# A retention layer with a gated MLP on one core: q decayed in its natural layout, one activation table at first, b_spatial as one row, and a new order of all work

## The chip, the core and the metric

The kernel runs on one core of one Trainium2 chip. The core has five engines, each of which works through its own queue in order: TensorE (matmuls and transposes, "PE" in the profile, with its weight loads as "PEld"), VectorE ("DVE"), ScalarE ("ACT"), GpSimd ("POOL") and SyncE ("SP", which here only issues DMAs). Data lies in HBM, in the on-chip SBUF, and in eight PSUM banks of 128 x 512 fp32 into which TensorE writes. The metric is the device time in microseconds (us), median over runs.

## The reference

Four batches, eight heads, 768 tokens, head size 64. Each head has a decay `lam` between 0.97 and 0.99. The first half is causal linear attention with decay; its output, with the heads laid side by side (512 wide), is the input `x` of a gated MLP that mixes tokens.

```python
# attention, per head: out_i = sum over j <= i of lam**(i-j) * (q_i . k_j) * v_j
# (the reference does it in blocks of 64 with a running state kv_state)
h = np.maximum(x @ w_in, 0.0)                    # 512 -> 1024
u, v = h[..., :512], h[..., 512:]
v_n = (v - mean(v)) / np.sqrt(var(v) + 1e-06)    # per token, over 512
v_s = np.einsum('ts,bsd->btd', w_spatial, v_n) + b_spatial[None, :, None]
out = (u * v_s) @ w_out                          # 512 -> 512
```

`w_spatial` is 768 x 768 and mixes all tokens of a batch. So no product with `w_spatial` can be finished before the attention, the first product and the normalisation of all 768 tokens of that batch are done.

## The kernel before

**Tiling.** A step n = 0..11 is 256 tokens of one batch (three steps a batch). Its q, k and v are 512 KB loads each (`load`, lines 191 to 194); a partition holds two neighbouring tokens. There are three buffers each for q, k and v, so the load of step n+3 waits until step n has been read. A step is two chunks c = 0, 1 of 128 tokens; heads are worked on in four pairs, in halves i (or x) = 0, 1.

**The decay** is split: k is multiplied by lam to the power (384 - t), q by lam to the power (t - 384), so the scores need only a 0/1 triangle, and the state in PSUM bank 7 is accumulated without being scaled. The factors are exp of log(lam) times a position. They exist in two forms: `lv` and `lqn` with tokens on partitions (for the natural layout), and `lq` with tokens along the free axis (for the transposed layout).

**The order is written out by hand**: the string `ORDER` (lines 16 to 84) is a list of tokens `name.arguments.engine`, and each token issues one helper's instructions at once; engine letters are T (TensorE), D (VectorE), A (ScalarE), P (GpSimd) and S (SyncE). Each engine's queue is the subsequence of its tokens, so a token that waits holds back all later tokens of its engine. Numbers behind the step are the PSUM banks. The tokens, in the order in which a step uses them:

| token | what it does | lines |
|---|---|---|
| lam, LB, LN, LL, LX, LT | load lam, spread it over partitions with a matmul, logarithm, exponents `lv`/`lqn`, the 12 rows of `lq` | 196 to 227 |
| one, FL | a tile of ones; k matmuls of ones into a bank, whose result nobody uses (filler) | 264 to 270 |
| LQ, LK, LV | load q, k, v of a step | 272 to 279 |
| KM, QM | decayed k (`kc`), decayed q (`qc`) in the natural layout, half a step each | 297 to 301 |
| QC | q copied to bf16 without decay (`qc`) | 284 to 287 |
| TK, TQ, EK, EQ | transposes on TensorE into a bank; eviction to `kT`, `qT`. EQ multiplies by `lq` | 317 to 337 |
| DK, DQ | the same transposes done by DMA | 303 to 309 |
| SC, MK, VC, KV, SS | scores, their mask into `a_sb`, v to bf16, state, state to SBUF | 311, 345 to 375 |
| AV, FN, EX | attention output for a chunk, one-element read between, eviction to `xT` | 377 to 419 |
| PV, EV, BN, RA, RD, VN | v half of x @ w_in, relu, statistics, sqrt, reciprocal, normalised `vn` | 421 to 454 |
| PU, EU | u half, transposed; relu into `uT` | 456 to 469 |
| WI, WS, WO, BS | loads of w_in (two halves), w_spatial (two halves), w_out on POOL's queue, cast to bf16 on the way; b_spatial copied to all 128 partitions on SP's | 247 to 261 |
| GT | POOL reads one element of a loaded q, k or v buffer, which holds POOL's queue until that load has landed | 244 |
| WT, EW | w_spatial transposed: `wt_sb` | 471 to 481 |
| GP, PW, GM | bias into a bank, the spatial product on top of it (6 matmuls of 384 columns), times `uT` into `gT` | 483 to 495 |
| PO, EO, ST | last product, eviction, 256 KB store; PH, EH, SH the same for half a tile | 497 to 522 |

In the order before, q of steps 0 to 4 is copied (QC) and gets its decay at the eviction of its transpose (EQ with `lq`); from step 5 on it is decayed in its natural layout (QM) and transposed by DMA (DQ). Steps 0 to 4 of k are decayed naturally and transposed on TensorE, later ones by DMA.

Of the kernel before, what the change touches and what calls it, by code (L numbers as in the profile page):

```python
# [25 lines left out]
FN.1.2.4.A AV.1.1.2.4.T LV.4.S EX.1.0.2.D EQ.2.1.5.D EX.1.1.4.A FL.13.256.1.0.T PV.1.0.1.T EX.0.0.3.D SS.1.1.D  # L26
PV.0.1.6.T EV.0.1.6.A PV.1.1.0.T EV.1.1.0.A KM.3.0.P KM.3.1.P QC.3.2.P GT.2.2.P WO.P EV.1.0.1.D BN.1.0.D
BN.0.1.D TK.2.0.2.T BN.1.1.D PV.0.0.5.T VC.3.P FL.3.256.4.0.T TK.2.1.4.T EK.2.1.4.D EK.2.0.2.A SC.2.0.0.1.T
MK.2.0.0.1.D FL.2.256.3.0.T SC.2.1.3.4.T MK.2.1.3.4.D EV.0.0.5.A RA.1.A BN.0.0.D RA.0.A RD.1.D LV.5.S RD.0.D
PU.1.0.6.T PU.1.1.2.T KV.2.0.T SS.2.0.A EU.1.0.6.A AV.2.0.0.1.T FN.2.0.1.D VN.0.0.D VN.0.1.D PU.0.1.3.T  # L30
EU.0.1.3.A KM.4.0.P AV.2.1.0.1.T EX.2.0.0.A EX.2.1.1.D GP.0.0.0.4.A EU.1.1.2.A GP.0.0.1.5.A PU.0.0.6.T VN.1.1.D
VN.1.0.D EU.0.0.6.D PV.2.0.3.T KM.4.1.P EV.2.0.3.A BN.2.0.D PV.2.1.0.T EV.2.1.0.A BN.2.1.D WT.0.0.1.T WT.1.0.2.T
EW.1.0.2.A EW.0.0.1.D RA.2.A RD.2.D VN.2.0.D WT.2.0.6.T EW.2.0.6.D PU.2.0.3.T GP.0.2.0.0.A PU.2.1.2.T VN.2.1.D
PW.0.0.0.4.T EU.2.0.3.A EU.2.1.2.A WT.1.1.1.T EW.1.1.1.A WT.2.1.6.T EW.2.1.6.A GP.0.3.0.3.D GM.0.0.0.4.D
GP.0.1.1.2.A PW.0.2.0.0.T GM.0.2.0.0.D GP.0.1.0.4.A WT.0.1.1.T EW.0.1.1.D PW.0.3.0.3.T TK.3.2.6.T EK.3.2.6.A
TQ.3.2.0.T PW.0.1.0.4.T GM.0.1.0.4.D EQ.3.2.0.D PW.0.1.1.2.T GM.0.1.1.2.D GM.0.3.0.3.D PW.0.0.1.5.T GM.0.0.1.5.D
KV.3.0.T SC.3.0.0.1.T MK.3.0.0.1.D SC.3.1.2.3.T MK.3.1.2.3.D GP.0.2.1.4.A PW.0.2.1.4.T TK.4.2.6.T QC.4.2.A
# [50 lines left out]
def kernel(  # L88
# [84 lines left out]
    def bank(b):  # L173
        return ps[:, b]
# [387 lines left out]
```

## Time and profile before

| | us |
|---|---|
| median of 3 runs (148.59 to 150.53) | 149.34 |
| span of the profiled execution, first to last instruction | 147.9 |
| PE busy / PEld / DVE / ACT / POOL in that span | 137.0 / 90.1 / 114.9 / 82.1 / 46.7 |
| chain that ended last: PE / DVE / ACT / issue / DMA / POOL | 81% / 6% / 4% / 4% / 1% / 1% |
| first matmul of PV (L424) / of PW (L488) | 21.77 / 36.47 |
| end of the last matmul / end of the span | 144.2 / 147.9 |
| HBM read and written | 24.77 MB and 6.29 MB |

The groups of the page give, for each source line and shape, the number of instructions, the engine's busy time and the mean duration of one. A TensorE matmul's listed duration includes a pipeline's depth, so the rate of a stream is read from the chain, where 4 PV matmuls take 0.86 us and 30 PW matmuls 4.88 us. Rows of waits name the instruction that waited, how long, and what ended it.

### The profile page before, as it was taken

The page shows a single profiled execution, that of the slowest core. Times are in us where ns is not written, and L with a number is a line of the kernel's source. Part 1 is how long each engine was busy: PE and PEld are TensorE (multiplying, and loading weights), DVE is VectorE, ACT ScalarE, POOL GpSimd, SP SyncE. Part 2 cuts the span into 40 slices and gives each one's busy share as a digit, 9 for nine tenths or more (in the row PEclk, how much of TensorE's full clock was granted, in tenths as well). Part 3 has the DMA queues.
Part 4 walks back from the last instruction along what each step waited for, and adds up shares of the span by engine and source line. Part 5 has one row for each costly group of instructions (what it writes and reads, how often), then busy time and mean ns, then how long its engine had stood idle before and what let it go on. Part 6 is the DMA issues. An engine that isn't in the chain of part 4 may idle for free.

```text
span 147.9 us, 4771 instructions
## 1 busy us (share of the span) xinstructions
PE 137.0 (93%) x2019; PEld 90.1 (61%) x2032; DVE 114.9 (78%) x216; ACT 82.1 (56%) x165; POOL 46.7 (32%) x59
## 2 busy tenths in 40 slices
PE   4999899999199999999999899999999999999990
PEld 2688675768076755556656647657665565666530
DVE  4458958988956998799998968797795899696720
ACT  3886635598066473786663367987424446742041
POOL 7594562019700080226041800780732000000000
PEclk9999999999999999999999999999999999999999
DMA  3999999999999005999998999999999579200524
GB/s 95 347 347 345 231 279 219 217 295 289 242 246 274 5 20 135 278 334 251 198 216 242 244 139 337 339 197 260 296 250 173 181 295 340 81 0 4 206 101 189
DMA packets 58376, 32.30 MB, mean 218 GB/s; under 512 B 15858, under 2 KB 55282, under 8 KB 58354
## 3 DMA queue, kind: packets, MB, share of 16 engines
q1 hardware_dynamic: 55968, 29.23, 74.2%
q0 software_dynamic: 2384, 2.75, 11.0%
q8 instruction: 16, 0.26, 0.7%
q14 instruction: 6, 0.05, 0.1%
q10 hardware_dynamic: 2, 0.00, 0.0%
HBM read 24.77 MB, written 6.29 MB: 210 GB/s over the span
## 4 chain that ended last, share of the span: by engine, by line
PE 81%; DVE 6%; ACT 4%; issue 4%; DMA 1%; POOL 1%; POOLq 0%
PE ps L488 21%; PE ps L424 13%; PE ps L499 12%; PE ps L462 11%; PE ps L269 6%; PE ps L399 4%; PE ps L352 4%; PE ps L369 4%; PE ps L321 3%; PE ps L390 2%; DVE a_sb L357 2%; DVE st L439 1%; DMA out_dram<-o_sb 1%; ACT uT L429 1%; ACT L220 1%
## 5 line engine op out<-in xcount | busy, mean ns | idle before, releaser
L488 PE MATMUL ps<-wt_sb,vn 128*128 128x384 bf16 x192 | 33.8, 326 | 3.0 <-DVE wt_sb L180 3.0
L291 POOL TENSOR_TENSOR kc<-k_in,lv 128x512 bf16<-128x512 f32 x18 | 19.1, 1072 | 39.2 <-DMA k_in<-in_k_dram 17.9
L357 DVE TENSOR_TENSOR a_sb<-ps,m 128x1024 bf16<-128x1024 f32 x24 | 28.7, 1215 | 2.6 <-PE ps L352 2.6
L488 PEld LDWEIGHTS <-vn 128*128 128x128 bf16 x192 | 18.2, 98 | 15.3 <-DVE vn L453 4.3
L462 PE MATMUL ps<-xT,win_sb 128*128 128x256 bf16 x192 | 23.5, 273 | 0.0
L424 PE MATMUL ps<-win_sb,xT 128*128 128x512 bf16 x92 | 22.6, 379 | 0.2
L499 PE MATMUL ps<-wout_sb,gT 128*128 128x512 bf16 x83 | 21.7, 380 | 0.7 <-issue 0.3
L494 DVE TENSOR_TENSOR gT<-ps,uT 128x384 bf16<-128x384 f32 x32 | 16.6, 550 | 6.3 <-PE ps L488 5.5
L462 PEld LDWEIGHTS <-win_sb 128*128 128x128 bf16 x192 | 18.1, 98 | 3.9
L439 DVE BATCH_NORM_STATS2 st<-vh 128x6 f32<-128x512 bf16 x24 | 16.5, 686 | 3.3 <-ACT vh L429 3.1
L178 ACT ACTIVATE ps<-bsp 128x384 f32<-128x384 f32 x26 | 12.5, 493 | 9.5 <-DVE gT L494 6.4
L291 POOL TENSOR_TENSOR qc<-q_in,lqn 128x512 bf16<-128x512 f32 x11 | 11.9, 1087 | 17.2 <-DMA q_in<-in_q_dram 10.3
L178 ACT ACTIVATE o_sb<-ps 128x512 f32<-128x512 f32 x18 | 10.5, 596 | 11.0 <-PE ps L499 10.4
L429 ACT ACTIVATE vh<-ps 128x512 bf16<-128x512 f32 x19 | 11.3, 595 | 8.8 <-PE ps L424 8.8
L269 PE MATMUL ps<-ones 128*128 128x256 bf16 x86 | 13.8, 309 | 2.0 <-DVE ones L265 1.5
L424 PEld LDWEIGHTS <-xT 128*128 128x128 bf16 x96 | 9.3, 98 | 9.5
L499 PEld LDWEIGHTS <-gT 128*128 128x128 bf16 x92 | 8.4, 98 | 9.1
L453 DVE TENSOR_SCALAR vn<-vh,mv,rstd 128x512 bf16<-128x512 bf16 x24 | 13.5, 592 | 0.2
L178 ACT ACTIVATE xT<-ps 128x512 bf16<-128x512 f32 x15 | 8.5, 595 | 7.4 <-PE ps L399 7.4
L178 ACT ACTIVATE s_sb<-ps 128x256 bf16<-128x256 f32 x17 | 6.5, 380 | 8.9 <-PE ps L369 8.8
L269 PEld LDWEIGHTS <-ones 128*128 128x128 bf16 x86 | 8.7, 109 | 4.3 <-DVE ones L265 1.5
L429 ACT ACTIVATE uT<-ps 128x512 bf16<-128x512 f32 x17 | 9.9, 588 | 1.7 <-PE ps L462 1.7
(72 smaller groups left out, 172.9 us busy)
## 6 DMA issues: line engine op xcount, KB each, us to landing
k_in<-in_k_dram SPq DMA_DIRECT2D x12, 512.0 KB, 6.1
q_in<-in_q_dram SPq DMA_DIRECT2D x12, 512.0 KB, 6.0
v_in<-in_v_dram SPq DMA_DIRECT2D x12, 512.0 KB, 6.7
out_dram<-o_sb SPq DMA_DIRECT2D x23, 256.0 KB, 2.7
wsp_raw<-in_moe_w_spatial_dram POOLq DMA_DIRECT2D x2, 576.0 KB, 11.4
win_sb<-in_moe_w_in_dram POOLq DMA_DIRECT2D x2, 512.0 KB, 9.9
wout_sb<-in_moe_w_out_dram POOLq DMA_DIRECT2D x1, 512.0 KB, 8.9
bsp<-in_moe_b_spatial_dram SPq DMA_DIRECT2D x1, 384.0 KB, 14.2
```

Of the source, the lines that this page charges most:

```text
L178: nc.scalar.activation(out=o, in_=i, func=AF.Copy)
L269: nc.tensor.matmul(out=bank(b)[:, 0:w], lhsT=ones[:, 0:P], rhs=ones[:, 0:w], start=(new == 1 and i == 0), stop=True, skip_group_check=True)
L291: vec(e).tensor_tensor(out=dst[n % NCA][:, u].rearrange("p u m o d -> p o (u m) d"), in0=src[n % NIN].rearrange("p (o u) m d -> p o u m d" ...
L357: nc.vector.tensor_tensor(out=a_sb[n % NA][:, i].rearrange("p o w j x -> p o w (j x)"), in0=ps[:, b0:b1 + 1:b1 - b0].rearrange("p o (w y) ...
L424: nc.tensor.matmul(out=bank(b), lhsT=x[:, slot(c, g)], rhs=win_sb[:, g, DH:DFF], start=(g == 0), stop=(g == NCH - 1))
L429: nc.scalar.activation(out=o, in_=i, func=AF.Relu)
L439: nc.vector.bn_stats(out=st6[p2][:, t], in_=vh[p2][:, t])
L453: vec(e).tensor_scalar(out=vn[p2][:, t], in0=vh[p2][:, t], scalar1=mv[p2][:, t, 0:1], scalar2=rstd[p2][:, t:t + 1], op0=ALU.subtract, op1= ...
L462: nc.tensor.matmul(out=pu[:, f2].rearrange("p (c x) -> p c x", c=2), lhsT=win_sb[:, g, f * P:(f + 1) * P], rhs=x[:, slot(0, g):slot(1, g) ...
L488: nc.tensor.matmul(out=bank(b)[:, 0:HW], lhsT=vn[bb % 2][:, s, f * P:(f + 1) * P], rhs=wt_sb[:, s, i * HW:(i + 1) * HW], start=False, stop ...
L494: nc.vector.tensor_tensor(out=gT[bb % 2][:, f, cols], in0=bank(b)[:, 0:HW], in1=uT[bb % 2][:, f, cols], op=ALU.mult)
L499: nc.tensor.matmul(out=bank(b), lhsT=gT[bb % 2][:, f, t * P:(t + 1) * P], rhs=wout_sb[:, f, :], start=(f == 0), stop=(f == NCH - 1))
```

## The change

It does four things. q is decayed in its natural layout in all twelve steps: QC, LT, `pos`, `lq` and `llrow` are gone, QM takes QC's place, and EQ becomes a plain copy that ScalarE can do too. One ScalarE table set that holds both logarithm and exponential is loaded before the logarithm (`tab.0.A`), and the set with the square root by a token of its own (`tab.1.A`). b_spatial is loaded as one row of 3 KB (BR) and spread over the partitions by two fp32 matmuls against a row of ones (BB), evicted by BE. And the whole order, with all bank numbers, is a new one; the fillers go from 86 matmuls of 256 columns to 13 of 512.

```diff
+    def c_tab(e, j):
+        nc.scalar.preload_act_table_set("sqrt_and_others" if j else "natural_log_exp_and_others")
+    def c_row(e):
+        nc.vector.memset(one_row, 1.0)
...
-    def b_sp(e):
-        nc.sync.dma_start(out=bsp, in_=moe_b_spatial.unsqueeze(0).to_broadcast((P, S)))
+    def b_r(e):
+        {"S": nc.sync, "A": nc.scalar}[e].dma_start(out=brow, in_=moe_b_spatial.unsqueeze(0))
+    def b_b(e, i, b):
+        nc.tensor.matmul(out=bank(b)[:, 0:HW], lhsT=one_row, rhs=brow[:, i * HW:(i + 1) * HW], start=True, stop=True)
+    def b_e(e, i, b):
+        copy(e, bsp[:, i * HW:(i + 1) * HW], bank(b)[:, 0:HW])
...
     def e_q(e, n, x, b):
-        nc.vector.tensor_tensor(out=qT[n % NTR][:, part(x)].rearrange("p u m x -> p (u m x)"),
-                                in0=quad(b)[:, part(x)].rearrange("p u m x -> p (u m x)"),
-                                in1=lq[:, n % NR, part(x)].rearrange("p u m x -> p (u m x)"), op=ALU.mult)
+        copy(e, qT[n % NTR][:, part(x)].rearrange("p u m x -> p (u m x)"),
+             quad(b)[:, part(x)].rearrange("p u m x -> p (u m x)"))
```

The order up to the first products with w_spatial, before and after:

```diff
-one.D lam.A LK.0.S msk.P mkc.D FL.6.256.0.1.T LB.0.T LN.0.A posk.P LL.D LX.A KM.0.0.D pos.P idn.P
-FL.11.256.1.1.T TK.0.0.1.T KM.0.1.P FL.5.256.2.1.T TK.0.1.2.T LQ.0.S QC.0.1.D TQ.0.1.3.T LT.0.A QC.0.0.P
-TQ.0.0.4.T EQ.0.0.4.D LT.1.A EQ.0.1.3.D LK.1.S KM.1.1.P FL.13.256.5.1.T TK.1.1.5.T EK.0.0.1.A SC.0.0.3.4.T
-EK.0.1.2.A LQ.1.S QC.1.0.P EK.1.1.5.A GT.1.1.P WI.0.P KM.1.0.D LV.0.S SC.0.1.0.1.T LV.1.S TK.1.0.6.T EK.1.0.6.A
-FL.1.256.2.0.T TQ.1.0.2.T LQ.2.S LK.2.S QC.1.1.P FL.11.256.5.0.T TQ.1.1.5.T MK.0.0.3.4.D EQ.1.0.2.D MK.0.1.0.1.D
-VC.0.A FL.3.256.6.0.T KV.0.0.T AV.0.0.3.6.T SS.0.0.A FN.0.3.6.A LV.2.S QC.2.1.P BS.S LK.3.S GT.1.2.P WI.1.P
-EQ.1.1.5.D SC.1.1.0.1.T SC.1.0.4.5.T MK.1.0.4.5.D KV.0.1.T SS.0.1.A KM.2.0.P GT.2.1.P WS.0.P LQ.3.S LT.2.A
-AV.0.1.3.6.T LV.3.S LK.4.S VC.1.D FL.13.256.2.0.T KV.1.0.T LQ.4.S SS.1.0.A FL.5.256.2.0.T KV.1.1.T KM.2.1.P
-LK.5.S MK.1.1.0.1.D AV.1.0.2.4.T QC.2.0.A TQ.2.1.5.T EX.0.1.6.D WS.1.P TQ.2.0.0.T EQ.2.0.0.D LQ.5.S VC.2.P
...
+lam.A idn.P row.D msk.P LB.4.T tab.0.A LN.4.A LQ.0.S LK.0.S LK.1.S LQ.1.S one.D FL.4.512.0.1.T posk.P LL.D LX.A
+mkc.D LV.0.S BR.S FL.2.512.4.0.T QM.0.0.P QM.0.1.D TQ.0.0.0.T KM.0.0.D LV.1.S KM.0.1.D TK.0.0.4.T TQ.0.1.2.T
+TK.0.1.1.T EQ.0.1.2.D EK.0.1.1.D SC.0.1.2.3.T EK.0.0.4.A EQ.0.0.0.A KM.1.0.P LQ.2.S KM.1.1.D QM.1.1.P
+MK.0.1.2.3.D TK.1.0.1.T TK.1.1.4.T SC.0.0.0.5.T MK.0.0.0.5.D FL.2.512.6.1.T WI.0.P LK.2.S FL.2.512.2.0.T
+BB.1.6.T EK.1.1.4.A VC.0.A AV.0.0.2.3.T KV.0.0.T VC.1.P LV.2.S QM.1.0.D LK.3.S SS.0.0.D TQ.1.1.0.T EQ.1.1.0.D
+TQ.1.0.5.T EK.1.0.1.A FN.0.2.3.A AV.0.1.2.3.T EX.0.0.2.A QM.2.1.P QM.2.0.P SC.1.1.0.1.T LV.3.S EQ.1.0.5.D
+SC.1.0.4.5.T BE.1.6.D EX.0.1.3.A MK.1.0.4.5.D KV.0.1.T SS.0.1.A KV.1.0.T SS.1.0.A FL.2.512.3.0.T TQ.2.1.3.T
+MK.1.1.0.1.D BB.0.4.T TQ.2.0.0.T FL.1.512.5.0.T KM.2.1.D EQ.2.0.0.A EQ.2.1.3.A AV.1.0.5.6.T FN.1.5.6.A GT.2.1.P
+WI.1.P KM.2.0.D KV.1.1.T TK.2.1.2.T TK.2.0.1.T EK.2.1.2.D GT.1.1.P VC.2.P AV.1.1.5.6.T EK.2.0.1.D SC.2.1.0.2.T
+SC.2.0.1.3.T BE.0.4.A EX.1.0.5.A SS.1.1.A EX.1.1.6.A PV.0.1.4.T LQ.4.S MK.2.0.1.3.D MK.2.1.0.2.D eps.D
+EV.0.1.4.A PV.0.0.5.T PV.1.0.3.T BN.0.1.D LQ.3.S EV.1.0.3.A tab.1.A KV.2.0.T AV.2.0.2.6.T WS.0.P PV.1.1.0.T
+EV.0.0.5.D FN.2.2.6.D SS.2.0.D BN.1.0.D AV.2.1.2.6.T PU.1.1.1.T GP.0.2.0.5.A EV.1.1.0.A EX.2.1.6.A EX.2.0.2.D
+KM.3.1.P KM.3.0.P PV.2.0.4.T GT.2.2.P WS.1.P PV.2.1.0.T EV.2.0.4.A TK.3.2.3.T PU.2.0.6.T BN.1.1.D BN.0.0.D
+RA.1.A RD.1.D VN.1.1.D VN.1.0.D WT.2.0.2.T WT.0.0.4.T LK.4.S RA.0.A RD.0.D EW.0.0.4.D VN.0.1.D VC.3.P BN.2.0.D
+EU.1.1.1.A EK.3.2.3.A PU.1.0.3.T EU.2.0.6.A EV.2.1.0.A QM.4.0.P GT.1.2.P QM.4.1.P KV.3.0.T PU.0.1.6.T WT.1.0.0.T
+BN.2.1.D EW.1.0.0.D PU.0.0.1.T EW.2.0.2.A RA.2.A LK.5.S TQ.4.2.2.T PU.2.1.0.T RD.2.D VN.2.1.D EU.1.0.3.A
+VN.0.0.D WT.1.1.4.T GP.0.1.0.3.A EU.0.1.6.A EU.0.0.1.A EQ.4.2.2.D EU.2.1.0.A VN.2.0.D PW.0.2.0.5.T GM.0.2.0.5.D
+GP.0.0.0.1.D PW.0.1.0.3.T WT.0.1.2.T WT.2.1.5.T WO.P GP.0.3.1.6.A QM.3.0.P QM.3.1.P LQ.5.S LV.4.S GM.0.1.0.3.D
...
```

In the middle of batch 1 the new order has on POOL, in a row, `QM.6.0 KM.7.1 QM.7.0 KM.7.0 VC.7` and then `QM.8.0 QM.8.1 KM.8.0 KM.8.1`; VN of steps 3 to 5 stands on VectorE among them. The last stores are those of the two halves of tile 5 of batch 3 (`PH EH SH`), where before they were those of whole tiles.

More of the change, by code (lines that the diff above doesn't have):

```diff
@@ L150 @@
     bsp = sb([P, S], FP32, "bsp")
+    brow = sb([1, S], FP32, "brow")
     ones = sb([P, 512], BF16, "ones")
@@ L215, in l_l @@
                                 in1=posk.unsqueeze(2).broadcast_to((P, NR, H, 2)), op=ALU.mult)
-        for o in range(2):
-            nc.vector.tensor_copy(out=llrow[row(o)], in_=loglam[row(o), 4 * o:4 * o + 4])
     def l_x(e):
@@ L221, in l_x @@
         nc.scalar.activation(out=lv, in_=lv, func=AF.Exp)
-    def l_t(e, r):
-        for u in range(4):
-            nc.scalar.activation(out=lq[:, r, u].rearrange("p m x -> p (m x)"),
-                                 in_=posq[:, r].rearrange("p m x -> p (m x)"), func=AF.Exp,
-                                 scale=llrow[:, u:u + 1])
     def c_ident(e):
@@ L240, in c_mask2 @@
             nc.vector.tensor_copy(out=m01[rows], in_=mfull[rows, :, :, rows])
-        nc.vector.memset(eps_t, 1e-6)
-        nc.vector.memset(one_row, 1.0)
     def after(e, x, n):
@@ L522, in st_o @@
         eng.dma_start(out=out[bb, t * P:(t + 1) * P, :], in_=o_sb[(bb * NT + t) % NO])
-    ops = dict(GT=after, one=c_ones, FL=f_l, FN=f_n, lam=c_lam, posk=c_posk, pos=c_pos, LB=l_b, LN=l_n, LL=l_l, LX=l_x, LT=l_t, idn=c_ident, msk=c_mask, mkc=c_mask2, WI=w_in, WS=w_sp, WO=w_out, BS=b_sp,
-               LK=ld_k, LQ=ld_q, LV=ld_v, KM=k_m, QM=q_m, DK=d_k, DQ=d_q, QC=q_c, VC=v_c, TK=t_k, TQ=t_q, EK=e_k, EQ=e_q,
+    ops = dict(GT=after, one=c_ones, FL=f_l, FN=f_n, lam=c_lam, posk=c_posk, tab=c_tab, row=c_row, eps=c_eps, LB=l_b, LN=l_n, LL=l_l, LX=l_x, idn=c_ident, msk=c_mask, mkc=c_mask2, WI=w_in, WS=w_sp, WO=w_out, BR=b_r, BB=b_b, BE=b_e,
+               LK=ld_k, LQ=ld_q, LV=ld_v, KM=k_m, QM=q_m, DK=d_k, DQ=d_q, VC=v_c, TK=t_k, TQ=t_q, EK=e_k, EQ=e_q,
                SC=s_c, MK=m_k, KV=k_v, SS=s_s, AV=a_v, EX=e_x, PV=p_v, EV=e_v, BN=b_n, RA=r_a, RD=r_d,
```

119 lines of the change are left out of this document (50 added, 69 removed).

## The prediction

> **What bounds the kernel now.** I read the page's bars first, then windows of the span, then the chain in order of time, then VectorE, POOL and the DMAs around the one gap.
>
> Two bars of the page, and two windows:
>
> ```profile
> PE   4999899999199999999999899999999999999990
> DMA  3999999999999005999998999999999579200524
> 20.10:40.24 20.14, 17.08 (x238) 12.06 (x229) 18.31 (x35) 11.53 (x22) 8.76 (x11) 1.00 1.11 251
> 40.24:144.20 103.96, 102.70 (x1479) 64.74 (x1489) 84.52 (x161) 57.04 (x114) 24.04 (x23) 1.00 0.80 201
> ```
>
> The columns of a window are its length, busy us of PE, PEld, DVE, ACT and POOL, the granted clock, the DMA share and GB/s. From 40.24 to 144.2 TensorE idles 1.26 us of 103.96: nothing an order does there wins much. In the 20 us ahead of it VectorE is busy 18.31 us, TensorE idles 3.06 us, and the DMA engines have no pause up to about 48 us.
>
> Of the chain (start, length, what it was) and, below, of VectorE's and POOL's timeline (start, length, engine, line) at the end of that window:
>
> ```profile
> 36.06 3.58 issue
> 39.64 0.56 DVE wt_sb L180
> 40.24 0.32 PE ps L488
> ...
> 35.73 0.79 POOL L258 DMA_DIRECT2D wout_sb<-in_moe_w_out_dram  x1
> 36.02 3.70 DVE L453 TENSOR_SCALAR vn<-vh,mv,rstd 128x512 bf16<-128x512 bf16 x1
> 36.52 1.05 POOL L182 CAST vb<-v_in 128x1024 bf16<-128x1024 f32 x1
> 37.52 2.04 POOL L291 TENSOR_TENSOR kc<-k_in,lv 128x512 bf16<-128x512 f32 x2
> ```
>
> This is the gap: a `vn` (VN, usually 0.41) takes 3.70 while POOL works without a break, and the first product with w_spatial (PW) stops after 4 matmuls. The steady part therefore starts at 40.24.
>
> The weights' loads in the list of DMA issues (last: median us to landing), and where they stand on POOL's timeline:
>
> ```profile
> win_sb<-in_moe_w_in_dram POOLq DMA_DIRECT2D x2, 512.0 KB, 9.9
> wsp_raw<-in_moe_w_spatial_dram POOLq DMA_DIRECT2D x2, 576.0 KB, 11.4
> ...
> 10.64 0.92 POOL L249 DMA_DIRECT2D win_sb<-in_moe_w_in_dram  x1
> 14.75 0.76 POOL L249 DMA_DIRECT2D win_sb<-in_moe_w_in_dram  x1
> 18.31 0.78 POOL L254 DMA_DIRECT2D wsp_raw<-in_moe_w_spatial_dram  x1
> 20.10 0.80 POOL L254 DMA_DIRECT2D wsp_raw<-in_moe_w_spatial_dram  x1
> 24.64 1.03 POOL L182 CAST vb<-v_in 128x1024 bf16<-128x1024 f32 x1 [3.74 <-PE ps L424]
> ```
>
> Asked one by one, these four loads land 9.4, 10.3, 10.5 and 12.3 us after issue: w_in at 20.1 and 25.1, w_spatial at 28.8 and 32.4. Loads of q, k and v landed every 1.5 us (4.9, 6.4, 7.9, 9.4, 10.9, 12.4, 13.9) until the weights' packets began at 14.5; v of step 2, issued at 10.93, then took 13.6 us, to 24.5.
>
> **The start.** Before, the first decay is at 6.19 behind Ln, a table load of 1.28 and two exponentials. After, q of step 0 is first on SP and lands when k did, at 4.9; lam's row is ready by then, with the table load under the wait for lam and `one_row` first on VectorE. That is 1.3 us earlier. It buys almost nothing: PV waits for w_in (first PV at 21.77, 13 fillers ahead of it), and WI.0 stands on POOL behind QM.1.1, which needs q of step 1: 9.4 + 1.04 = 10.5, against 10.64.
>
> **What goes away.** The 12 rows of `lq` (L225, 5.0 us) leave ScalarE, which is idle in 8.6 of the 20 us ahead of 40.24: worth nothing by itself. QM instead of QC and EQ costs VectorE or POOL 0.68 or 1.04 a half where the copies cost 0.6 to 1.3: even. b_spatial's 384 KB leave SP's queue, 1.1 us at 512 KB per 1.5 us, behind v of step 2, so no load in front of it gains. No row shows an fp32 matmul of 384 columns. LB (L208) shows that an fp32 matmul is two passes, and 0.61 us for 8 columns. So each of the two new ones costs at least 0.16 (one PW matmul) and at most about 1.25 (LB's 0.61 and two passes of 384 columns at the slow fillers' 0.32); I take 0.6, nearest to LB, the only fp32 row. With their evictions (0.55 and 0.49) they run ahead of 20.1, where TensorE waits for w_in; without that cover they cost 1.2 together. The fillers fall from 86 x 0.109 = 9.4 us to 13 x 0.216 = 2.8. They lie in waits, so nothing is won: the waits stay.
>
> **The attention of step 2 moves ahead of PV.** Its MK (2.35), EK and EQ are now done by about 22, while w_in is awaited. What VectorE keeps between w_in's landing and the first PW is 1 EV 0.68, 6 BN 5.2, 1 EX 0.69, SS 0.42, 2 EW 1.1, EQ 0.68, 6 VN 2.4, RD 0.5: 11.7 us in place of 18.3. VectorE is no bound there any more, and in the order TensorE could reach PW at 20.1 + 5.2 (PV) + 5.2 (PU) + 3 (attention, transposes) = 33.5.
>
> **But w_spatial comes later.** POOL's queue reads now: WI.0, VC.1, QM.2.1, QM.2.0, GT, WI.1, GT, VC.2, WS.0, KM.3.1, KM.3.0, GT, WS.1. Before, both WS stood ahead of VC.2 and KM.3. Queued behind VC.2's wait are thus both halves of w_spatial. q of step 2 lands at 13.9; two QM of 1.04 and GT put WI.1 at 16.3 (was 14.75), landing 10 later at 26.3. VC.2 waits for v of step 2: 20 at the earliest (three 1.5 us slots past 13.9 and the weights' part), 24.5 as before at the latest; the weights' second burst begins 1.5 later, so I take 22. VC.2 1.04, then WS.0 issued at 23.1 (was 18.31). Before, WS.0 waited its turn behind WI.1; now it does not, so I take w_out's 8.9: landing at 32.0 (was 28.8). Range 29.9 to 35.0 (24.5 + 1.04 + 9.4). WS.1 is issued after two KM and lands 3.6 behind, at 35.6, the distance it had before.
>
> In TensorE's queue WT.2.0 and WT.0.0 need WS.0; behind them stand 4 PU (3.5), KV 0.24, TQ of step 4 0.44, and WT.1.0 and WT.1.1 0.33 each: with WT.2.0 and WT.0.0 5.5 us to the first PW, and WS.1 has landed when it is reached. VectorE's queue has EW.0.0, which needs WT.0.0, ahead of VN.0.1, two BN, EW.1.0, RD, VN, VN, EQ, VN: 4.7 us after 32.7, so both arrive together near 37.5. TensorE waits about 1.5 for WI.1 at PU.1.1 and 2 for WS.0 on the way. I add 0.5 for a VN behind a single POOL instruction (1.17 and 0.87 instead of 0.41 at 67.57 and 96.55): PW starts at 38.0.
>
> **The rest.** From 40.24 the kernel before took 103.94 to its last matmul. After 38.0, TensorE has 4 PW matmuls more (0.65) and 6 transposes of w_spatial (0.33), TK.3 and TQ.4 (0.44 each) and KV.3.0 (0.24) fewer: 103.1. I leave its 2.5 us of waits as they were (103.94 less 101.45 of work by the chain's rates), bounds 0 and +5, since all of the order is new. The tail: before 3.7 (last o_sb 0.60, store 2.0, 1.1 to close); after, the last is half a tile: 0.38, a half store's 2.0, 1.1: 3.5. Sum 38.0 + 103.1 + 3.5 = 144.6 of span. The median stands 1.45 above the profiled span: 146.1.
>
> **The rivals.** *w_spatial early* (15%): v of step 2 lands at 20, WS.0 at 30, PW at 35.5: 35.5 + 103.1 + 3.5 + 1.45 = 143.6. For it: WI.1 begins later. Against: v took 13.6 us.
>
> *POOL holds VN* (slower, 13%). The hold of 36.02 went over three POOL instructions and w_out's issue. POOL now also has 19 QM in place of 11. If VN is held for whole bursts, then batch 0 loses 3.3 (w_out and two QM stand by VN.0.1 to VN.2.0, where VectorE and TensorE arrive together), and batch 1 up to 5.2, less the 1.0 of one instruction, at QM.6.0, KM.7.1, QM.7.0, KM.7.0, VC.7. With w_spatial at 34: 146.1 + 2.0 + 2.8 + 4.2 = 155; with w_spatial as forecast 153.1. Batch 0 alone gives 148.9, so it ends above 149.34 once batch 1 loses over 0.4, and over 2% slower from 3.4: a burst of four instructions whose data has landed. The Trainium skill, "SBUF — State Buffer", section "Who interferes with whom", has a lock per instruction: the second one in waits till the first has finished. The hold of 1.17 agrees, the 3.70 does not; by that rule batch 0 and 1 lose at most one instruction per VN and the forecast stands.
>
> *The clock stays low* (10%). The first fillers ran at 0.213 us per 256 columns, and at 0.109 only from 8.3. With few fillers TensorE's first 20 us are mostly transposes and gaps. If the clock is still half at 20.1, PV and PU run at twice 0.87 until it rises, some 6.8 us (1.5 to 8.3 before): 3.4 lost, less what the waits for WI.1 and WS.0 cover; if a wait lets it fall again before PU, 3.5 more, uncovered: 149.6. Against: the gap of 2.96 at 40.24 left it at 1.00. The Trainium skill, "TensorE: Matmul & The Clock Gate", Part 1, puts the fall at an idle window of about 3.4 us; my waits of 1.5 and 2 stay below it, and by that rule nothing is lost.
>
> *The saving is given back later* (17%): the new order of the middle or VectorE's evictions cost 2 to 3 more: 148.6.
>
> **How the numbers follow.** The forecast as such has 45%, centred on 146.1 with about 2 either way (w_spatial 1.5 either way, the middle 1). 2% is 3.0 us, about what a measurement of this kernel can tell from no change (its runs spread 1.3%): faster below 146.35, slower above 152.3. A little over half of the forecast (0.26) and the early case (0.15) are faster, with 0.03 of the given-back case where the middle gets shorter instead: 0.44. Slower: most of the POOL case (0.11) and 0.03 of the clock's: 0.14. Same: 0.42. The range is 142.8 (early case, with 0.8 of the middle's waits gone) to 150.8 (the clock and half of the POOL case).
>
> **What would show it.** Right: w_spatial's first load issued at 22 to 25.5, landing at 30.5 to 34; VectorE well under 18 us busy in 20 to 40; first PW at 37 to 39; the steady part as long as before. Wrong: PW at 40 or later; `vn` of 2 us and more; matmuls of PV at 0.21 x 2 apart; a part behind PW over 106 us.

## The result, and the profile after

The changed kernel takes 164.7 us (163.9 to 165.5) where the kernel before takes 149.4 (148.6 to 150.5): 1.103 times the time, 95% interval 1.097 to 1.108. The forecast was 146.1, with a range that ended at 150.8. The profiled execution took 163.9, its span is 161.9. Times are medians over all executions of a kernel. Some executions are over 1.5% slower than the fastest of their kernel: ratios use the others alone, four experiments have too few of those for a ratio, and the traces of aligned buffers alone (168.18) and of the three kernels with w_spatial earlier (154.45, 150.56 and 151.92) are of slower ones, so what these four show is not shown of the faster ones.

The two bars of the page and two windows of the changed kernel, with the columns of the windows before (length, busy us of PE, PEld, DVE, ACT, POOL, clock, DMA share, GB/s):

```profile
PE   4588999899987879899796949999695969999990
DMA  3999999999989299999997799886247106425066
20.10:40.24 20.14, 19.16 (x321) 13.55 (x325) 16.73 (x36) 13.55 (x28) 10.18 (x13) 1.00 1.17 265
40.31:158.00 117.69, 102.97 (x1447) 63.38 (x1456) 86.47 (x163) 52.30 (x110) 29.29 (x29) 1.00 0.75 177
```

From the first PW (40.31) to the last matmul TensorE now takes 117.69 us for 102.97 of work: it idles 14.7 us where it idled 1.26. The bar shows where: the slices of 4 to 7 lie all over the part that had been solid. The unbroken run of PWs begins where it began before (40.31 against 40.24). The page's chain by engine and by line:

```profile
PE 68%; DVE 20%; DMA 3%; ACT 3%; issue 3%; SPq 0%; DVEq 0%
PE ps L479 17%; PE ps L490 11%; DVE a_sb L348 11%; PE ps L415 11%; PE ps L453 8%; PE ps L343 4%; PE ps L390 4%; PE ps L313 3%; DMA k_in<-in_k_dram 3%; PE ps L360 3%; DVE vn L444 3%; DVE st L430 2%; PE ps L381 2%; PE ps L255 1%; PE ps L266 1
```

VectorE's part of the chain rose from 6% to 20%, and more than half of it is one line, L348, the mask multiply MK (2% before, as L357). VectorE is not busier: 113.6 us in all, against 114.9. Somebody waits for MK who did not before.

The gap of before, a VN of 3.70 in front of the first PWs, is gone. On VectorE and POOL at the same place:

```profile
38.68 1.46 DVE L444 TENSOR_SCALAR vn<-vh,mv,rstd 128x512 bf16<-128x512 bf16 x2
...
38.84 2.20 POOL L283 TENSOR_TENSOR qc<-q_in,lqn 128x512 bf16<-128x512 f32 x2 [1.73 <-DMA q_in<-in_q_dram]
```

And the weights' loads on POOL's timeline. w_spatial's first half is issued at 24.35, behind VC.2, and lands 9.4 later, at 33.7:

```profile
11.58 0.93 POOL L240 DMA_DIRECT2D win_sb<-in_moe_w_in_dram  x1
18.22 0.80 POOL L240 DMA_DIRECT2D win_sb<-in_moe_w_in_dram  x1
23.36 1.04 POOL L178 CAST vb<-v_in 128x1024 bf16<-128x1024 f32 x1 [4.16 <-DMA v_in<-in_v_dram]
24.35 0.75 POOL L245 DMA_DIRECT2D wsp_raw<-in_moe_w_spatial_dram  x1
```

### The profile page after: what moved, and what is told of

The parts are those of the page before. It is cut to its first block, busy times and chain, and to the rows that moved or that the text cites. A ratio compares the mean times of both kernels' runs of the same rounds, so it can differ in the third digit from the quotient of the medians.

```text
span 161.9 us, 4600 instructions
## 1 busy us (share of the span) xinstructions
PE 137.2 (85%) x1947; PEld 85.9 (53%) x1963; DVE 113.6 (70%) x216; ACT 72.8 (45%) x150; POOL 50.2 (31%) x61
## 4 chain that ended last, share of the span: by engine, by line
PE 68%; DVE 20%; DMA 3%; ACT 3%; issue 3%; SPq 0%; DVEq 0%
PE ps L479 17%; PE ps L490 11%; DVE a_sb L348 11%; PE ps L415 11%; PE ps L453 8%; PE ps L343 4%; PE ps L390 4%; PE ps L313 3%; DMA k_in<-in_k_dram 3%; PE ps L360 3%; DVE vn L444 3%; DVE st L430 2%; PE ps L381 2%; PE ps L255 1%; PE ps L266 1%
## 5 line engine op out<-in xcount | busy, mean ns | idle before, releaser
L348 DVE TENSOR_TENSOR a_sb<-ps,m 128x1024 bf16<-128x1024 f32 x24 | 29.1, 1222 | 9.7 <-PE ps L343 3.0
L283 POOL TENSOR_TENSOR kc<-k_in,lv 128x512 bf16<-128x512 f32 x16 | 16.5, 1046 | 36.2 <-DMA k_in<-in_k_dram 16.5
L283 POOL TENSOR_TENSOR qc<-q_in,lqn 128x512 bf16<-128x512 f32 x19 | 20.4, 1084 | 22.8 <-DMA q_in<-in_q_dram 16.1
L174 ACT ACTIVATE ps<-bsp 128x384 f32<-128x384 f32 x23 | 11.3, 495 | 16.3 <-DVE a_sb L348 8.3
L174 ACT ACTIVATE xT<-ps 128x512 bf16<-128x512 f32 x19 | 10.8, 595 | 15.0 <-PE ps L390 13.1
L174 ACT ACTIVATE o_sb<-ps 128x512 f32<-128x512 f32 (+1 forms) x14 | 8.1, 578 | 13.9 <-PE ps L490 10.9
L444 DVE TENSOR_SCALAR vn<-vh,mv,rstd 128x512 bf16<-128x512 bf16 x24 | 11.4, 503 | 0.3
L420 ACT ACTIVATE uT<-ps 128x512 bf16<-128x512 f32 x20 | 11.3, 589 | 0.3 <-PE ps L453 0.3
L178 POOL CAST vb<-v_in 128x1024 bf16<-128x1024 f32 x7 | 7.3, 1037 | 13.2 <-DMA v_in<-in_v_dram 5.8
L390 PE MATMUL ps<-a_sb,vb 64*64 64x128 bf16 x384 | 10.8, 225 | 0.3 <-issue 0.3
L343 PE MATMUL ps<-qT,kT 64*64 64x128 bf16 x384 | 10.2, 233 | 0.5 <-DVE kT L176 0.5
```

The source lines that it names most:

```text
L174: nc.scalar.activation(out=o, in_=i, func=AF.Copy)
L283: vec(e).tensor_tensor(out=dst[n % NCA][:, u].rearrange("p u m o d -> p o (u m) d"), in0=src[n % NIN].rearrange("p (o u) m d -> p o u m d" ...
L343: nc.tensor.matmul(out=pa[o][row(c), w, j], lhsT=kT[n % NTR][row(o), u, j, c * Q64:(c + 1) * Q64], rhs=qv(n, o, u, c), start=(w == 0 and j ...
L348: nc.vector.tensor_tensor(out=a_sb[n % NA][:, i].rearrange("p o w j x -> p o w (j x)"), in0=ps[:, b0:b1 + 1:b1 - b0].rearrange("p o (w y) ...
L390: nc.tensor.matmul(out=po[c ^ o][row(w), c, i], lhsT=vb[n % NCA][row(c), 4 * o + u, j, :], rhs=a[row(c), i, o, w, j, :], start=(r == 0 and ...
L420: nc.scalar.activation(out=o, in_=i, func=AF.Relu)
```

## Who waits for the mask multiply

A stretch of the changed kernel's timeline (start, length, engine, line; in brackets the idle time before it and what ended it), with a line from ten us later:

```profile
45.75 1.23 DVE L348 TENSOR_TENSOR a_sb<-ps,m 128x1024 bf16<-128x1024 f32 x1 [0.52 <-PE ps L343]
...
47.03 1.14 PE L479 MATMUL ps<-wt_sb,vn 128*128 128x384 bf16 x6 [0.31 <-DVE a_sb L348]
...
48.20 1.23 DVE L348 TENSOR_TENSOR a_sb<-ps,m 128x1024 bf16<-128x1024 f32 x1 [0.17 <-PE ps L479]
...
49.48 0.61 PE L313 MATMUL ps<-ident,kc 128*128 128x128 bf16 x8 [1.32 <-DVE a_sb L348]
...
57.84 1.02 PE L490 MATMUL ps<-wout_sb,gT 128*128 128x512 bf16 x4 [1.55 <-DVE a_sb L348]
```

The order has, there, `MK.3.0.2.5 ... PW.0.0.1.3 ... MK.3.1.0.4 ... TK.4.2.1`, and later `MK.4.0.3.6 ... PO.0.3.5` (numbers at the end are banks). None of these shares a bank or a tile with the MK it waits for. PW in bank 3 waits for an MK of banks 2 and 5; the next MK, of banks 0 and 4, waits for that PW in bank 3; the transposes into bank 1 wait 1.32 for the MK of 0 and 4; PO in bank 5 waits 1.55 for an MK of 3 and 6. Each time the bank lies *between* the MK's two. The line that does it is in both kernels:

```python
in0=ps[:, b0:b1 + 1:b1 - b0].rearrange("p o (w y) -> p o w y", w=2)
```

All eight banks are one tile, `ps`, and MK reads two of them as a strided slice. The waits are as if the slice covered everything from b0 to b1. Before, the two banks of all 24 MKs are neighbours, and nothing lies between; in the new order this holds for 5, and the banks in between add up to 42 over the 24. I call these false waits.

**The multiply cut in two.** One instruction for each bank:

```diff
-            in0=ps[:, b0:b1 + 1:b1 - b0]...   # one tensor_tensor over both banks
+        for o, b in ((0, b0), (1, b1)):
+            nc.vector.tensor_tensor(out=a_sb[n % NA][:, i, o]..., in0=bank(b)..., ...)
```

> The changed kernel with the mask multiply MK cut into two instructions, one for each of its two PSUM banks. Nothing else differs. Theory (false waits): MK reads its two banks as one strided slice of the single tile ps, and the slice counts as everything from the first bank to the second; in the changed order 19 of 24 MKs have one to four banks between their two, and whoever uses those banks waits for MK. In the trace of the changed kernel a transpose into bank 1 waits 1.32 us for an MK of banks 0 and 4 (at 49.5), a last product in bank 5 waits 1.55 for an MK of banks 3 and 6 (at 57.8). Cut in two, no bank is between: the part after the first product with w_spatial falls from 117.7 us to 104 to 108, TensorE's waits for a_sb on L479, L490, L415 and L313 vanish, and the time is 150 to 154. Rival (the order itself): VectorE holds too much at the wrong places in the new order whatever the banks are; then 24 more instructions on VectorE (about 0.14 us each, 3.4 us) make it 164 to 168. Rival (the clock and the loads of the start): the part ahead of 40 us is unchanged and so is the rest, 164 to 165.

Measured: 152.65 (152.28 to 154.19), 1.023 times the kernel before (1.016 to 1.030), as expected. TensorE's time from the first PW to the last matmul:

```profile
40.34:146.67 106.33, 103.98 (x1454) 63.88 (x1455) 87.01 (x180) 51.59 (x108) 28.82 (x28) 0.98 0.84 194
```

The first PW is where it was (40.34 against 40.31). The part behind it had grown by 13.7 us (117.69 against 103.96); 11.4 of them are back, and TensorE idles 2.35 us in it. Who waited for the line (us, times), in the kernel before, in the changed kernel, and here:

```profile
  ACT ps L178: 2.9, 2
  POOL qc L182: 1.9, 1
  PEld L369: 0.4, 1
```

```profile
  ACT ps L174: 8.3, 4
  PE ps L479: 4.4, 6
...
  PE ps L490: 2.9, 2
...
  PE ps L415: 2.2, 1
...
  PE ps L313: 1.3, 1
```

```profile
  ACT ps L174: 3.9, 3
  PEld L480: 0.2, 1
```

No TensorE matmul waits for MK any more. The order itself holds little up.

**The same instructions, other bank names.** Every bank number in the order goes through one fixed permutation, so each bank keeps its users and their turn (an MK's two banks are named lower one first), and only what lies between an MK's two banks changes. Banks 0 to 6 become 1 2 4 5 0 3 6 (few between), 6 3 2 0 1 4 5 (many), and in the kernel before 4 1 6 0 3 5 2:

```diff
 changed kernel     MK.3.0.2.5  MK.3.1.0.4  TK.4.2.1
-few                MK.3.0.3.4  MK.3.1.0.1  TK.4.2.2
+many               MK.3.0.2.4  MK.3.1.1.6  TK.4.2.3
```

> The changed kernel with its banks 0 to 6 renamed by one fixed permutation throughout: the same instructions in the same order, every bank with the same users in the same turn. Only what lies between the two banks of an MK changes: 15 of 24 MKs have neighbouring banks (5 in the changed kernel), and the banks in between sum to 21 (42 there). Theory (false waits): about half of the loss of 14 us goes, 155 to 160. Rival (the order itself): bank names mean nothing, 164 to 165. Rival (start): 164 to 165.

> The changed kernel with its banks 0 to 6 renamed by another fixed permutation: the banks in between sum to 62 (42 in the changed kernel), one MK of 24 has neighbouring banks. Theory (false waits): slower than the changed kernel, 168 to 176. Both rivals: 164 to 165.

> The kernel before, whose 24 MKs all have neighbouring banks, with its banks 0 to 6 renamed by one fixed permutation after which none has and the banks in between sum to 65. Same instructions, same order, same users of every bank. Theory (false waits): the kernel before loses as the change did or more, 160 to 175 in place of 149. Rival (the new order alone has the loss): 149 to 150.

| kernel | banks in between, sum over 24 | time | ratio to before (95%) |
|---|---|---|---|
| changed, MK per bank | 0 | 152.65 | 1.023 (1.016 to 1.030) |
| changed, few between | 21 | 157.23 | 1.050 (1.044 to 1.057) |
| changed | 42 | 164.7 | 1.103 (1.097 to 1.108) |
| changed, many between | 62 | 178.25 | 1.187 (1.177 to 1.198) |
| before | 0 | 149.4 | 1 |
| before, many between | 65 | 189.19 | 1.265 (1.256 to 1.275) |

The two upper bounds were set too low (176 and 175), the direction is the theory's in all three. That the kernel before, in its own order, loses 40 us by renaming its banks leaves nothing for the rival that bank names mean nothing. Not all of the 40 is waiting: the granted clock of these executions was 0.927 to 0.945. Three of its four longest waits of TensorE (us in total, times, longest) have MK as their releaser; the other ends with a bias copy of ScalarE (GP), and these copies themselves waited 11.6 us for MK:

```profile
PE ps L499 <- DVE a_sb L357: 6.0, 4, 2.3
PE ps L488 <- ACT ps L178: 5.9, 2, 3.0
PE ps L424 <- DVE a_sb L357: 5.8, 2, 3.3
PE ps L462 <- DVE a_sb L357: 3.3, 2, 2.0
```

## The 3 us that are left: the address of the load buffers

With MK per bank the kernel is still 2.3% slower than before. GB/s in 40 slices of the first 20 us, before and then changed:

```profile
GB/s 0 0 0 6 59 161 333 350 345 346 347 345 347 351 344 346 347 345 347 351 344 346 347 345 347 351 344 378 326 279 209 211 215 213 217 235 318 359 369 292
```

```profile
GB/s 0 0 0 11 83 92 329 346 339 295 287 288 295 289 290 288 294 288 291 292 288 289 293 293 290 290 288 291 291 291 289 291 291 279 209 205 219 214 215 254
```

The same loads of q, k and v move at 347 GB/s before and at 290 after, 1.49 and 1.80 us for each 512 KB. The change took `posq`, `posqi`, `lq` and `llrow` out of SBUF, 12,320 B of a partition with llrow's 16 rounded to 32: 24 x 512 + 32. All tiles declared behind them moved down by that; `brow` (6 x 512) moved those behind it up again by whole multiples. So, apart from whole multiples of 512 B, the load buffers now begin 480 B past where they began. No view shows the addresses: "on a multiple of 512 B" stands in the texts below for "where they began in the kernel before", and is assumed. (The sizes declared ahead of the weights there, each rounded up to 32 B, add up to 15,232 B, which is 384 past a multiple.) An unused tile puts the change right, or does the same to the kernel before:

```diff
+    pad = sb([P, 8], FP32, "pad")       # 32 B; 120 elements (480 B) in the first run
     win_sb = sb([P, NCH, DFF], BF16, "win_sb")
```

> The kernel before with one unused tile of 480 B per partition declared ahead of the weights' tiles, so that all load buffers begin 480 B past a multiple of 512, as they do in the changed kernel by the removal of posq, lq and llrow (before: on a multiple of 512). Nothing else differs. Theory (address of the load buffers): the 512 KB loads of q, k and v of the first 15 us come every 1.80 us instead of 1.49 (290 instead of 347 GB/s), the packets of 512 B take 34 ns instead of 27, the first PW comes 1 to 2 us later, and the time is 150 to 152. Rival (the order of the loads on the queue, q first, sets their rate): 1.49 us each, 149.3 to 149.7.

> The changed kernel with MK per bank, and one unused tile of 32 B per partition declared ahead of the weights' tiles, after which all load buffers begin on a multiple of 512 B. Theory (address of the load buffers): the loads come every 1.49 us, v of step 2 lands near 20.5 instead of 22.9, w_spatial's first half near 31.5 instead of 33.7, the first PW starts near 38.5 instead of 40.3, and the time is 150 to 151.5 (152.65 without the tile). Rival (order of the loads): no change, 152.3 to 153.

> The kernel before with one unused tile of 32 B per partition, so that all load buffers begin 32 B past a multiple of 512 B. Asked is only the rate of the first loads. Reading 1 (any start off a multiple of 512 costs the same): 34 ns a packet and 1.80 us a load, as with the shift of 480 B. Reading 2 (it depends on where the 512 B fall): between 27 and 30 ns, 1.49 to 1.6 us. The Trainium skill, DMA: Bandwidth & Descriptors, section How a descriptor splits into AXI transactions, has pieces of 256 B that start on multiples of 256, with unused bytes still moved; by an estimate from its rule, if it holds for the writing side, a start 480 B past needs 23 beats instead of 16 and a start 32 B past 17, which would be reading 2.

The kernel before shifted by 480 B takes 150.86, ratio 1.009 (1.005 to 1.014), as expected. The changed kernel with MK per bank and the tile of 32 B, called aligned from here on, takes 149.54, ratio 0.997 (0.993 to 1.001), where it was 1.023: the theory's side, a little below its 150 to 151.5. Their rates, shifted first, then aligned, and last the kernel before shifted by 32 B:

```profile
GB/s 0 0 0 13 96 87 346 347 332 293 289 289 292 292 286 291 291 290 290 293 288 291 290 293 289 290 289 289 293 289 306 282 230 211 217 220 213 217 213 283
```

```profile
GB/s 0 0 0 11 126 110 343 348 346 345 347 345 349 348 346 345 347 345 349 352 342 346 347 345 349 348 345 346 347 289 206 215 207 226 209 240 315 358 326 336
```

```profile
GB/s 0 0 0 10 104 118 317 348 337 297 293 286 291 293 290 288 292 291 290 289 293 290 286 294 291 289 290 291 291 287 292 309 283 254 211 212 209 220 213 216
```

Rate and address change together, in both orders. Shifted by 32 B (one execution, 151.26) the loads also come at 290 GB/s: reading 1. Both shifts are off every multiple of 64, 128 and 256 B too, so which boundary counts stays open. By an estimate from the Trainium skill, "DMA: Bandwidth & Descriptors", "How a descriptor splits into AXI transactions", whose rule is about reads, a shift of 32 B would have cost one beat in 16 if the buffers began on a multiple of 256 and the rule held for the side that is written; the row shows the full loss, so the measurement decides against that reading.

What the rate is worth in time is less plain. The first PW of the aligned kernel came at 39.39, only 0.95 earlier than without the tile and not near 38.5; the part behind it took 103.7 in place of 106.3, at a granted clock of 1.00 in place of 0.98. The tile also moves every other tile declared behind it. So the loads' rate is shown to hang on the shift, and the time on the tile; that the rate accounts for all of the 3 us is not shown.

## The start: clock and w_spatial

In the changed kernel the first fillers of 512 columns came every 0.43 us, where 4 PV matmuls of 512 columns take 0.86 in the steady part, and BB's two passes took 1.64 at first and 0.91 later: TensorE ran at half its rate until some point between. (The row of the granted clock on the profile's page reads full from the start and does not show it; the spacing of the matmuls does.)

```profile
14.25 1.64 PE L255 MATMUL ps<-brow,one_row 1*128 1x384 f32 x2
...
21.53 0.91 PE L255 MATMUL ps<-brow,one_row 1*128 1x384 f32 x2
```

Six more fillers in the first 7 us:

```diff
-row.D msk.P LB.4.T ... one.D FL.4.512.0.1.T
+one.D row.D msk.P FL.3.512.0.1.T LB.4.T ... FL.7.512.0.1.T
```

> As mask_per_bank_aligned, with six more filler matmuls of 512 columns in the first 7 us (three ahead of LB, three more behind it). Theory (clock): TensorE's clock is granted in full from about 8 us as in the kernel before, instead of 13 to 20, the attention of steps 0 and 1 runs at full rate, and 0.5 to 1.5 us are won. Rival: the first PV waits for w_in anyway, within 0.4 of mask_per_bank_aligned.

147.48, ratio 0.984 (0.978 to 0.990): some 1 to 2% faster than the kernel before, and 1.3% (1.9 us) below the aligned kernel without the six (0.997). TensorE's timeline has BB at the full rate at once, and the first PV 3.7 us earlier than without the six (24.23):

```profile
11.16 0.91 PE L256 MATMUL ps<-brow,one_row 1*128 1x384 f32 x2
...
20.52 1.69 PE L417 MATMUL ps<-win_sb,xT 128*128 128x512 bf16 x6
```

The fillers do not decide this alone. With MK per bank and neither tile nor fillers, BB ran at the full rate at 13.42, and the first PV came at 23.28:

```profile
13.42 0.91 PE L255 MATMUL ps<-brow,one_row 1*128 1x384 f32 x2
```

Over all traces of the new order, BB's first pair took 0.91 in each of the six that have the fillers; in the seven without them it took 0.91 to 1.07 in three and 1.64 or 1.65 in four. Two of these seven have the same instructions up to that point and differ all the same (1.65 at 13.04, 1.07 at 12.95). In one trace with the fillers the rate was low again at BB's second pair (1.11 at 16.72). So the fillers make an early full rate likely, and what one start is worth rests on a single trace each.

**The parts one by one in the changed kernel.** MK is over two banks again in the first three; the fourth has new bank numbers, dealt out so that all 24 MKs have neighbours (`MK.3.0.4.5 MK.3.1.2.3 TK.4.2.6`).

> The changed kernel with the unused tile of 32 B per partition that puts all load buffers on a multiple of 512 B, and MK as it is, one instruction over two banks. Theory (two separate losses, false waits about 12 us and the address of the load buffers about 3): the loads come every 1.50 us, the first PW starts near 39, the part behind it stays as long as in the changed kernel (117.7 us), time 161.5 to 163. Rival (they cover each other): 164 to 165, because the false waits take up what the earlier start gives.

> The changed kernel with only the six more fillers of aligned_more_fillers: MK over its two banks as it is, load buffers where they are. Theory (three separate losses: false waits, address, clock): TensorE's clock is granted in full from 6 to 8 us in place of 20.2, and the time is 1 to 2.5 us less than the changed kernel's 164.7: 162 to 163.7. Rival (the clock alone is worth nothing while the loads are late and MK holds others): 164.2 to 165.2.

> The changed kernel with the unused tile of 32 B and the six more fillers, MK over its two banks as it is. Against neighbour_banks_aligned_fillers (148.5) only the bank numbers differ. Theory (separate losses): the false waits alone are left, about 12 us: 159.5 to 161.5, with TensorE's waits for a_sb on other banks' work of 10 us or more. Rival (part of the loss of the changed kernel lay in the clock, half until 20.2 us, and comes with it): under 158.

> The order of the changed kernel with its bank numbers given out anew so that the two banks of every MK are neighbours (MK stays one instruction over both), with the unused tile of 32 B and with the six more fillers of aligned_more_fillers. Theory (false waits): no bank is ever between, so it is as fast as aligned_more_fillers (147.5) or faster by what the 24 further VectorE instructions cost there (up to 0.14 us each): 146 to 147.5, and below the kernel before (149.3). Rival (splitting helped for another reason, such as shorter MKs): over 149.

| changed kernel with | time | ratio (95%) |
|---|---|---|
| aligned buffers | 162.4 to 168.2 | none |
| six fillers | 164.64 | 1.106 (1.097 to 1.115) |
| both | 163.58 | 1.096 (1.086 to 1.106) |
| both, neighbouring banks | 148.49 | 0.992 (0.989 to 0.995) |

The last two rows differ in bank numbers alone (but for a flag of four fillers that starts their bank anew): 15.1 us, the whole loss. Alignment and fillers are worth 5.2 us once the false waits are gone (152.65 to 147.48), and some 1 us while they last (1.103 against 1.096, intervals that overlap), though the first PW does move from 40.31 to 38.25 with both. So the parts don't add up, and the expectations that they would missed, for both together (159.5 to 161.5) and for the fillers alone (162 to 163.7), where the rival's 164.2 to 165.2 holds. Aligned alone stays open: in its profile BB's passes are slow even longer, and the first PW comes at 42.74. That neighbouring banks would be at least as fast as MK per bank (147.48) was not borne out either; the new numbers also change which work reuses which bank, and I have not taken that apart.

**w_spatial earlier.** The prediction held that WS behind VC.2 on POOL's queue sets the first PW. Three runs have it earlier. The first has MK per bank, aligned buffers and no added fillers; the other two have neighbouring banks and the fillers (17 tokens have other bank numbers than in the kernel that they are compared with, no MK among them), and in the second w_out's load (`WO`) also stands behind QM.3, in the third behind KM.4.

```diff
-WI.1.P ... GT.1.1.P VC.2.P ... WS.0.P ... KM.3.1.P KM.3.0.P ... GT.2.2.P WS.1.P
+WI.1.P ... GT.1.1.P WS.0.P VC.2.P WS.1.P ... KM.3.1.P KM.3.0.P ... GT.2.2.P
```

> As mask_per_bank_aligned, and w_spatial's two loads moved up in POOL's queue: the first ahead of VC.2, the second right behind VC.2 instead of behind KM.3. Theory (the prediction's term: w_spatial behind VC.2 sets the first PW): w_spatial's first half lands near 28.5 and the second near 31, PW starts 1 to 2 us earlier than in mask_per_bank_aligned, time 1 to 2 us less. Rival (TensorE and VectorE are as late by themselves: in the changed kernel with MK per bank TensorE was busy 13.9 of the 16 us ahead of the first PWs): within 0.5 of mask_per_bank_aligned, or more because v of step 2 lands later.

> As neighbour_banks_aligned_fillers, with w_spatial's first half ahead of VC.2 in POOL's queue, its second half right behind VC.2, and w_out's load (WO) behind QM.3 instead of ahead of it. In aligned_w_spatial_early w_spatial's first half landed 2.2 us earlier than without, but one VN took 4.05 us from 36.5 on, beside w_out's issue and three POOL instructions behind it. Theory (the prediction's term, w_spatial behind VC.2 sets the first PW): with that VN at 1.3 us or less PW starts 1 us or more earlier than in neighbour_banks_aligned_fillers, and the time is 0.5 to 1.5 us less. Rival (TensorE and VectorE are as late by themselves, and v and q of step 3 come later): within 0.5 us, or slower.

> As neighbour_banks_aligned_fillers, with w_spatial's first half ahead of VC.2 and its second right behind VC.2 in POOL's queue, and w_out's load behind KM.4, that is behind the first PWs, so that no VN stands beside it. Theory (the prediction's term, w_spatial behind VC.2 sets the first PW): no VN over 1.3 us ahead of the first PW, w_spatial's first half lands near 29 instead of 31.5, PW starts at 37.5 or earlier instead of 38.1, 0.5 to 1.5 us less than neighbour_banks_aligned_fillers (148.5). Rival (v and q of step 3 come later, and TensorE and VectorE are as late by themselves): the same within 0.5, or slower.

w_spatial's first half landed at 29.3, 28.8 and 29.0 in place of 31.5, and in these traces the first PW came later each time: 40.94, 40.53 and 40.51, against 39.39 and 38.11 without the move. The third has a ratio, 1.000 (0.995 to 1.005), where the kernel with w_spatial late has 0.992 (0.989 to 0.995); the first two have none. In the third, VectorE and POOL ahead of the first PW, and the PW:

```profile
36.52 3.92 DVE L445 TENSOR_SCALAR vn<-vh,mv,rstd 128x512 bf16<-128x512 bf16 x2
...
35.57 3.03 POOL L284 TENSOR_TENSOR qc<-q_in,lqn 128x512 bf16<-128x512 f32 x3
38.57 1.03 POOL L284 TENSOR_TENSOR kc<-k_in,lv 128x512 bf16<-128x512 f32 x1
...
40.51 1.81 PE L480 MATMUL ps<-wt_sb,vn 128*128 128x384 bf16 x6 [2.16 <-DVE vn L445]
```

v of step 3 now landed behind w_spatial, at 32.9 (26.6 without the move), so POOL's work piled up into one burst just where the VNs stand, and the first of these two VNs took 3.23. By the ratio the rival was right that an earlier w_spatial wins nothing. Its reason is not shown: PW waited 2.16 for the held VN, and without that wait it would have stood near 38.35, by an estimate, where it stood without the move (38.11). Whether the move wins anything where no VN is held stays open.

## Why the prediction was wrong

**The step that failed** is "I leave its 2.5 us of waits as they were ... bounds 0 and +5, since all of the order is new". The part behind the first PW measured 117.7, not 103.1. I compared orders token by token and priced every move, but read bank numbers as names; 19 of 24 MKs had moved their banks apart, and the slice in `m_k` stood in the listing. The bound of +5 had no row behind it. In the place of these waits the runs showed false waits for MK: 15.1 us between two kernels that differ in bank numbers (163.58 and 148.49). The case "saving given back later" named the right place with 2 to 3 us, a fifth of it, and with another mechanism, so it was no more than a lucky direction.

**The sum of the miss.** Of 18.6 us (164.7 less 146.1), the first PW gave 2.3 (40.3 against 38.0), the part behind it 14.6, the tail 0.4 (3.9 against 3.5) and the distance of the median from the span 1.35 (2.8 against 1.45). The range's upper end does not come out of what it names either: the clock (3.5) and half of the POOL case (half of 7.0) on top of 146.1 make 153.1, not 150.8. Even that would have been far below 164.7.

**The first 40 us** went by the steps, each late: WI.0 issued at 11.6 (forecast 10.5), WS.0 at 24.35 (23.1), landing at 33.7 (32.0), PW at 40.3 (38.0). I had put loads at 1.49 us each from the kernel before, and TensorE at its full rate; with MK per bank, aligned buffers bring the first PW to 39.39, and the six fillers on top to 37.73. "VectorE is no bound there any more" did not hold either: it was busy 16.73 us from 20.10 to 40.24, and the chain from 35.43 to 41.20 is all its own, 5.8 us where the forecast had 4.7. With buffers aligned, six fillers and neighbouring banks the same order gives 10.60, 21.74, 31.5 and 38.1, and this stretch from there to its last matmul:

```profile
38.11:142.58 104.47, 102.11 (x1447) 63.22 (x1456) 85.57 (x162) 52.37 (x109) 28.58 (x28) 1.00 0.77 199
```

104.5 for a forecast of 103.1. The order is what I took it for; the kernel that carried it was not.

**Fillers worth nothing**: in the changed kernel as it is, yes (164.64 with six more). Once the false waits are gone, some 2 us (0.997 against 0.984): in the two traces the low rate moved the first PV from 20.5 to 24.2, by stretching the attention in front of it. The clock rival thus had the low rate right and its place wrong: it put the loss on PV and PU, but the changed kernel's first 11 PV matmuls took 2.76 at 25.27, the full rate.

**BB** was put at 0.6 each, bounds 0.16 and 1.25: 0.91 at the full rate, and 1.64 at half, outside the bounds, which did not allow for that.

**POOL holds VN** did not happen in the changed kernel (VNs of at most 1.15 us). But such holds exist beyond the kernel before, as the trace of the last experiment shows: 3.23 us over three POOL instructions, with no DMA issue ahead of it. I had discounted it by the Trainium skill, "SBUF — State Buffer", "Who interferes with whom", which has the second one in wait for one instruction. Holds of 1.1 agree with that; the 3.23 here and the 3.70 before do not.

**w_spatial sets the first PW**: its landing was 1.7 later than forecast, within the range of 29.9 to 35.0; its rank differs from kernel to kernel. With MK per bank alone the chain in front of the first PW does run through it, from its issue to its landing at 33.68:

```profile
24.03 9.65 DMA wsp_raw<-in_moe_w_spatial_dram
```

In the changed kernel and in the aligned one the chain runs over TensorE's and VectorE's own work there: in the changed kernel TensorE was busy 19.16 of the 20.14 us in front of 40.24, and moving w_spatial ahead in the kernel with neighbouring banks won nothing.

## What to carry to other kernels

A slice that skips over part of a tile may be tracked as the whole stretch it spans: keep what one instruction reads together next to each other, or give separate tiles, and when an order or an allocation is made anew, look at bank numbers as at waits. After any change of what is allocated, look at where the load buffers begin; here 32 B more in front made the loads 1.20 times as fast (290 to 347 GB/s). Read the first rows of "who waited for it" for the line whose share of the chain rose, and ask of each waiter which data it shares with that line; if none, the wait is false.

## What the runs showed of the hardware

- Loads in packets of 512 B into SBUF ran at 347 GB/s with the buffers where the kernel before has them, and at 290 with buffers 32 or 480 B past that, the 480 B in two orders of the loads. Which boundary counts was not tried.
- A VN beside back-to-back POOL instructions was held for one of them (1.1 to 1.3 us in most cases) or for the whole burst (3.70 before, 4.05 in the first run with w_spatial earlier and in the kernel before with its banks renamed, 3.23 in the third with w_spatial earlier). What decides between the two is open.
- TensorE's rate in the first 20 us differed between traces of the new order: with six more fillers BB's first pair took 0.91 in six of six, without them 0.91 to 1.07 in three of seven and 1.64 or 1.65 in four. The first PV of the aligned kernel came at 20.52 with them and at 24.23 without.
